# Two V tiles moved from the stage before the attention scores into the filler work between them, the first keys fetched on ScalarE's queue, and another order of the last output tiles

## The chip, the cores and the metric

One core of a Trainium2 chip runs the whole program in one launch. The metric is the device time of one execution in microseconds (us), measured three times; beside it stands one profiled execution, from which all rows below are taken. TensorE is PE in the profile, VectorE DVE, ScalarE ACT, GpSimd POOL and SyncE SP. SP does no arithmetic here; it issues almost all transfers.

## The reference

The input x is 2048 x 512, in float32. The output mixes an attention part and a gated feed-forward part by a gate for each row:

```python
qkv = (x @ wqkv)                      # split into q, k, v: 32 heads of 16 columns each
p = softmax(q @ k.T * 16 ** -0.5)     # 2048 x 2048 for each head
a = (p @ v) @ wo
b = (silu(x @ w1) * (x @ w3)) @ w2    # inner width 1792
g = sigmoid((x * gate_w).sum(-1))
out = g * a + (1 - g) * b
```

## The kernel before

**Precision.** Every float32 product outside the softmax is made of three matmuls on a high and a low half (hi x hi, hi x lo, lo x hi). A V tile (128 rows of x times the V part of `wqkv`, four blocks of 128 inputs) is thus 12 matmuls, in `sums_v`, called by `project_v` (ScalarE copies the result to `V`) or directly.

**The stage before the scores** makes the halves of x, q and k of the first eight heads (stored to DRAM, `store_qk`, and read back by `load_q` and `load_k` into `Qt` and `Kt` with the rows in the order that the score matmuls want), and the 16 V tiles. It also bounds all scores (`bound`), writes the bound to DRAM as guard rows (`guard_rows`, tensor `m_d`) and reads them back under the queries (`load_guard`). A flag from the bound decides at L293 whether a slow exact path (`row_maxima`) is needed. With these inputs it isn't, so every engine jumps over it.

**The branch.** Each engine loads the flag, compares, and jumps. On the path that is taken each engine first waits for its own earlier instructions, and then adds to its semaphores what the skipped path would have added. SP does this for the transfers: it waits until all transfers issued so far have landed, whichever queue issued them, and then counts the eight transfer semaphores up, one after the other. The first score matmul (L829) waits for these counts. Transfers take the eight semaphores (DMAHW0 to DMAHW7 in the rows below) in turn, in the order of the built program with all queues together; one that takes a semaphore waits at its queue until the transfer that had it before has landed.

**The scores.** 1024 units follow, each one score pair (`Q`, two matmuls side by side on 50 rows, L829) and one exponential on ScalarE (L833); the product with V (`P`, L817) comes eight units at a time. Between them stand filler slots (`F`): in one slot `feed` issues one matmul on each half of the array (64 rows each, side by side) from a list of blocks, `blocks()`: the other q and k columns, the feed-forward part, the output projection. A string sets the order. A period `one` has 8 Q, 21 F and 8 units of P, a period `two` 8 Q, 15 F and 8 units of P:

```python
LONG, SHORT = 90, 37
one = "QQFFFFFF" + "QFFF" * 5 + "QPPPP"
two = "QFFF" * 5 + "QPPQQPP"
order = one * LONG + "QQ" + "F" * 7 + two * SHORT + "QFFF" * 5 + "QPPPP"
```

**The end.** After the last P the last two heads are divided by their sums through two rounds of transposes, split into halves, and multiplied with the last block of `wo` (`project`). `mix` then forms `g * a + bt` of one 128-row tile on VectorE and stores it. Output tiles 8 to 15 finish in this stage; of tiles 8 and 10 the scaling runs on ScalarE and the sum on GpSimd (`scaled`).

Of the kernel before, what the change touches and what calls it, by code (L numbers as in the profile page):

```python
# [17 lines left out]
P = 128  # L18
# [4 lines left out]
DH = 16  # L23
NB = S // 512
# [9 lines left out]
def gated_mix_kernel(ctx: ExitStack, tc: tile.TileContext, x, wqkv, wo, w1, w3, w2, gate_w, out):  # L34
# [27 lines left out]
    qkp = ctx.enter_context(tc.tile_pool(name="qkp", bufs=1))  # L62
    fw = ctx.enter_context(tc.tile_pool(name="fw", bufs=2, side="right"))
# [3 lines left out]
    wvp = ph1.enter_context(tc.tile_pool(name="wvp", bufs=1))  # L67
# [330 lines left out]
    bound()  # L398
    project_v(10)
    guard_rows()  # L400
    load_k(0, 0)
    project_v(11)
    x_gate(3)
# [118 lines left out]
    def load_piece(t, q):  # L522
        if t == 1 and q < 2:
            both = wk.tile([P, 2, 512], F32R, name=f"wo{2 + q}")
# [9 lines left out]
    def load_wo(k):  # L534
        if k < 2:
            hi, lo = w2H[3][:, 2 + k, :], w2L[3][:, 2 + k, :]
        else:
            both = wk.tile([P, 2, 512], F32R, name=f"wo{k}")
# [66 lines left out]
    def divide(k, half):  # L605

        yield from reciprocals(k, half)
        for b in (2 * half, 2 * half + 1):
# [4 lines left out]
            else:  # L613
                both = wk.tile([P, 2, 512], F32, name="od")
# [12 lines left out]
    def load_bt(t):  # L627
        bt[t] = wk.tile([P, 512], F32, name=f"bt{t % 3}")
# [62 lines left out]
    def six_heads():  # L691
# [9 lines left out]
        both = wk.tile([P, 2, 512], F32, name="od")  # L701
# [36 lines left out]
    NBLOCK = 8 * len(chunks) + 3 * NT + NT // 2 + NT // 2  # L738
# [4 lines left out]
    halves = [None, None]  # L743
# [7 lines left out]
    def pick(lane, rest, gap):  # L751
# [3 lines left out]
        if used < 0 or over[used] is not None and over[used] + rest <= clock:  # L755
            block, halves[lane] = halves[lane] or next(source, None), None
            if block:
                if type(block[1]) is tuple:
                    product, done, length = block
                    block, halves[1 - lane] = (product, done[0], length), (product, done[1], length)  # L760
                over.append(None)
                return dict(block=block, ps=bank(), id=len(over) - 1, n=0, turn=None, alone=halves[1 - lane] is not None or len(over) == NBLOCK)
# [78 lines left out]
    LONG, SHORT = 90, 37  # L841
# [7 lines left out]
    for i, c in enumerate(order):  # L849
        clock += 1 if c != "P" else 4  # L850
        if c == "Q":
# [14 lines left out]
            if small or later and hurry:  # L866
                for _ in range(3 if hurry else 1 + (len(small) > (6 if len(over) < 8 * len(chunks) - 16 else 0))):
                    if small or later and hurry:
                        (small or later).pop(0)()
            if loads and (hurry or issued % 2 or len(over) > 8 * len(chunks) - 12):  # L870
                loads.pop(0)()
# [44 lines left out]
    project(last, 1, (0, 1))  # L916
# [8 lines left out]
    project(last, 1, (2,))  # L925
    project(last, 2)

    def scaled(t):
        y = wk.tile([P, 512], F32, name=f"p{free[t // 2 - 3]}")
        nc.scalar.activation(y, banks[t], AF.Copy, scale=g[:, t:t + 1])  # L930
        nc.gpsimd.tensor_add(bt[t], bt[t], y)

    def store(t):
        nc.sync.dma_start(out[P * t:P * t + P, :], bt[t])

    banks[8], banks[9] = one_[:, 1, :], two_[:, 1, :]
    banks[10], banks[11] = bank(), bank()
    for two in ((8, 9), (10, 11), (12, 13), (14,), (15,)):
        if two[0] == 12:
            banks[12], banks[13], banks[14] = psum2()[:, 0, :], psum2()[:, 0, :], acc  # L940
        for terms in ((0, 1), (2,)):
            for t in two:
                project(t, k, terms)
        for t in two:
            if t in (8, 10):
                scaled(t)
            elif t < last:
# [33 lines left out]
```

## Time and profile before

| | before |
|---|---|
| median of three runs | 1403.72 us (1402.86 to 1403.92) |
| the profiled execution | 1403.71 us |
| its span in the profile | 1401.9 us |
| PE busy | 1393.8 us, 99% of the span |
| ACT busy | 1034.3 us, 74% |
| DVE busy | 486.9 us, 35% |
| POOL busy | 329.3 us, 23% |
| bytes moved by the DMA engines | 141.03 MB |

The span runs from the first to the last recorded instruction; 1.8 us of the execution lie around it. Matmuls are pipelined and their ends are modelled, so PE's 99% says that it seldom stands idle, not that it runs at its peak.

### The profile page before, as it was taken

Reading aid. Unit: us, or ns where it says so; the run is one execution under the profiler, and the core shown is the slowest. Engines: PE = TensorE matmul, PEld = TensorE weight load, DVE = VectorE, ACT = ScalarE, POOL = GpSimd, SP = SyncE. Lnnn points to the kernel's source line nnn. Section 1 sums busy time; section 2 is a strip of 40 time slices with the busy share of each in tenths; the row PEclk is TensorE's granted clock in tenths of the full one; section 3 lists DMA queues with packets and bytes.
Section 4 is the critical chain, followed back from the end, with each engine's and each line's share of the span. In section 5 each row is a group of like instructions: output and inputs, shape, how many; then the busy total and the mean of one; then the engine's idle time right before and its main releaser. Section 6 shows DMA issues by size and latency. Waiting matters only on the chain.

```text
span 1401.9 us, 29019 instructions
## 1 busy us (share of the span) xinstructions
PE 1393.8 (99%) x11497; PEld 826.4 (59%) x11497; DVE 486.9 (35%) x1083; ACT 1034.3 (74%) x1155; POOL 329.3 (23%) x366
## 2 busy tenths in 40 slices
PE   9999999999999999999999999999999999999998
PEld 8866566566566566566566566566555555555554
DVE  5511111564555546555454554511111101111113
ACT  4457677777777777777777777777677887888784
POOL 6123433011011101110110116432344322212312
PEclk9999999999999999999999999999999999999999
DMA  7653554343223423223333236444354453444632
GB/s 209 166 124 94 133 139 113 73 113 77 46 56 85 114 54 76 69 66 93 74 77 74 66 86 165 118 95 91 87 123 105 105 110 77 111 93 110 157 120 78
DMA packets 112479, 141.03 MB, mean 101 GB/s; under 512 B 16276, under 2 KB 70804, under 8 KB 109264
## 3 DMA queue, kind: packets, MB, share of 16 engines
q1 hardware_dynamic: 111616, 137.92, 41.4%
q8 instruction: 93, 1.52, 0.5%
q10 hardware_dynamic: 720, 1.18, 0.2%
q14 instruction: 50, 0.41, 0.1%
HBM read 90.43 MB, written 48.61 MB: 99 GB/s over the span
## 4 chain that ended last, share of the span: by engine, by line
PE 99%; DVE 0%; issue 0%; DVEq 0%
PE acc L817 33%; PE f L432 27%; PE S L829 19%; PE f L550 11%; PE f L634 2%; PE S L199 2%; PE f L641 1%; PE f L96 1%; PE f L98 1%; PE f L97 1%; PE f L165 0%; PE acc L353 0%; PE f L897 0%; PE S L165 0%; PE S L897 0%; DVE xL L646 0%
## 5 line engine op out<-in xcount | busy, mean ns | idle before, releaser
L833 ACT ACTIVATE p<-S 128x1024 f32<-128x1024 f32 x1024 | 967.9, 1026 | 314.1 <-PE S L829 305.0
L817 PE MATMUL acc<-p,V 128*17 128x512 f32 x4096 | 471.5, 594 | 0.0
L829 PE MATMUL S<-Qt,Kt 50*128 50x512 f32 x2048 | 403.7, 407 | 0.8 <-DVE V L415 0.8
L829 PEld LDWEIGHTS S<-Qt,Kt 50*128 50x128 f32 x2048 | 184.0, 184 | 173.5 <-issue 77.7
L817 PEld LDWEIGHTS acc<-p,V 128*17 128x17 f32 x4096 | 103.4, 97 | 275.2 <-issue 275.2
L463 DVE RECIPROCAL sg<-sg 128x64 f32<-128x64 f32 x448 | 209.2, 517 | 52.7 <-issue 49.1
L432 PE MATMUL f<-xH,fl 64*128 64x512 f32 x1088 | 220.6, 395 | 0.0
L432 PE MATMUL f<-xL,fh 64*128 64x512 f32 x1088 | 219.6, 393 | 0.0
L432 PE MATMUL f<-xH,fh 64*128 64x512 f32 x1088 | 218.0, 389 | 0.0
L328 POOL CAST fh<-fr 128x512 fp32r<-128x512 f32 x34 | 22.4, 658 | 428.0 <-DMA fr<-in_B_w_dram 279.6
L432 PEld LDWEIGHTS f<-xH,fh 64*128 64x128 f32 x1088 | 105.6, 184 | 25.0 <-issue 0.4
L432 PEld LDWEIGHTS f<-xL,fh 64*128 64x128 f32 x1088 | 106.4, 186 | 22.5
L432 PEld LDWEIGHTS f<-xH,fl 64*128 64x128 f32 x1088 | 106.1, 186 | 22.7
L789 DVE MEMSET tick<- 1x1 f32 x198 | 11.7, 59 | 281.2 <-PE f L550 143.0
L455 DVE COPY gs<-f 128x512 f32<-128x512 f32 x56 | 38.5, 688 | 65.5 <-PE f L432 59.3
L461 DVE TENSOR_SCALAR sg<-sg 128x512 f32<-128x512 f32 x56 | 27.3, 488 | 88.0 <-ACT sg L460 84.3
L550 PE MATMUL f<-xH,fh 64*128 64x512 f32 x208 | 57.5, 392 | 0.0
L550 PE MATMUL f<-xH,raw 64*128 64x512 f32 x192 | 57.0, 392 | 0.0
L550 PE MATMUL f<-xL,fh 64*128 64x512 f32 x208 | 56.2, 392 | 0.0
L550 PE MATMUL f<-xH,fl 64*128 64x512 f32 x208 | 55.4, 392 | 0.0
L513 POOL CAST fh<-sg 128x512 fp32r<-128x512 f32 (+1 forms) x32 | 18.0, 563 | 147.3 <-DMA sg<-h_d 91.0
L799 DVE COPY u<-acc 128x512 f32<-128x512 f32 x31 | 21.4, 692 | 86.1 <-PE acc L817 86.1
(202 smaller groups left out, 1324.6 us busy)
## 6 DMA issues: line engine op xcount, KB each, us to landing
Kt<-kH_d SPq DMA_DIRECT2D x128, 128.0 KB
h_d<-sg SPq DMA_DIRECT2D x56, 256.0 KB
sg<-h_d SPq DMA_DIRECT2D x43, 256.0 KB
fr<-in_B_w_dram SPq DMA_DIRECT2D x42, 256.0 KB
Qt<-qH_d SPq DMA_DIRECT2D x128, 64.0 KB
Kt<-kL_d SPq DMA_DIRECT2D x64, 128.0 KB
Qt<-qL_d SPq DMA_DIRECT2D x64, 64.0 KB
b_d<-y SPq DMA_DIRECT2D x16, 256.0 KB
```

The source lines that it names most:

```text
L199: nc.tensor.matmul(ps[:, i, :], w[i][h][:, k, :], xs[b][:, k, :], start=n == 0, stop=n == len(order) - 1)
L328: nc.gpsimd.tensor_copy(hi, src)
L432: return nc.tensor.matmul(ps, w[i == 1][r, k, :], (xL if i == 2 else xH)[b][r, k, :], start=n == 0 and not second, stop=n == 3 * ND - 1 an ...
L455: nc.vector.tensor_copy(gs, ps)
L461: small.append(lambda: nc.vector.tensor_scalar(sg, sg, 1.0, None, op0=OP.add))
L463: small.append(lambda q=q: nc.vector.reciprocal(sg[:, q:q + 64], sg[:, q:q + 64]))
L550: ins = nc.tensor.matmul(ps, hs[t][q][i == 1][r, P * o:P * o + P], (w2L if i == 2 else w2H)[q][r, o, :], start=n == 0 and not second, stop ...
L634: return nc.tensor.matmul(ps, ot[t][i == 1][r, P * k:P * k + P], wo_[k][i == 2][r, :], start=n == 0 and not second, stop=n == 3 * ND - 1 a ...
L799: nc.vector.tensor_copy(u, acc)
L817: nc.tensor.matmul(acc[r:r + DH + 1, :], V[:, k, 2 * j + h, :], p[:, h, :], start=k == 0, stop=k == NT - 1)
L829: nc.tensor.matmul(ps[:, h, :], Kt[i][r:r + 50, P * k:P * k + P], Qt[i][r:r + 50, t:t + 512], start=True, stop=True)
L833: nc.scalar.activation(p, ps, AF.Exp, scale=SCALE)
```

## The change

The diff, cut to its core:

```diff
+EARLY = 14
...
-    def x_gate(b):
-        for t in range(4):
+    def x_gate(b, ts=range(4)):
+        for t in ts:
...
-            vh, vl = (wvp.tile([P, 512], F32R, name=f"v{n}{k}") for n in "hl")
+            both = wvp.tile([P, 2, 512], F32R, name=f"v{k}")
+            vh, vl = both[:, 0, :], both[:, 1, :]
...
-    def load_k(j, i):
+    def load_k(j, i, e=nc.sync):
...
-                nc.sync.dma_start(Kt[i][r + DH * o:r + DH * o + DH, :].bitcast(F32), QD[1][ks][s, :])
+                e.dma_start(Kt[i][r + DH * o:r + DH * o + DH, :].bitcast(F32), QD[1][ks][s, :])
...
     bound()
+    x_gate(3, range(3))
     project_v(10)
     guard_rows()
-    load_k(0, 0)
+    load_k(0, 0, nc.scalar)
+    x_gate(3, range(3, 4))
     project_v(11)
-    x_gate(3)
...
     load_guard(0, 0, 0)
-    project_v(12)
     small = nc.values_load(flag, min_val=0, max_val=1)
-    last_v = [sums_v(t) for t in range(NT - 3, NT)]
+    last_v = [sums_v(t) for t in range(12, EARLY)]
...
+    def v_product(t):
+        b, o = divmod(P * t, 512)
+        def product(ps, r, n, second):
+            k, i = divmod(n, 3)
+            return nc.tensor.matmul(ps, (xL if i == 1 else xH)[b][r, k, o:o + P], wv[k][i == 2][r, :],
+                                    start=n == 0 and not second, stop=n == 3 * ND - 1 and second)
+        return product
+
+    def v_done(t):
+        return lambda ps: nc.vector.tensor_copy(V[:, t, :, 0:DH], ps.rearrange("p (h d) -> p h d", d=DH))
...
+        for t in range(EARLY, NT):
+            yield v_product(t), v_done(t), 3 * ND
         for m, b in turns:
...
-        for t in range(NT // 2, NT - 2):
+        for t in range(NT // 2, NT - 3):
             yield part_product(t, True), part_done(t), LATE
-        yield part_product(NT - 2, False), (part_done(NT - 2), part_done(NT - 2)), LATE
+        for t in (NT - 3, NT - 2):
+            yield part_product(t, False), (part_done(t), part_done(t)), LATE
...
-        if used < 0 or over[used] is not None and over[used] + rest <= clock:
+        if used < 0 or over[used] is not None and over[used] + (rest if len(over) < NBLOCK - 3 else 3) <= clock:
...
-    LONG, SHORT = 90, 37
+    LONG, SHORT = 94, 33
...
-    project(last, 1, (0, 1))
+    project(last, 1)
...
-    project(last, 1, (2,))
-    project(last, 2)
+    project(last, 2, (0, 1))
     banks[8], banks[9] = one_[:, 1, :], two_[:, 1, :]
     banks[10], banks[11] = bank(), bank()
-    for two in ((8, 9), (10, 11), (12, 13), (14,), (15,)):
...
+    project(8, k, (0, 1))
+    project(last, 2, (2,))
+    project(8, k, (2,))
+    mix(8, banks[8])
+    for t in range(9, NT):
+        if t == 12:
             banks[12], banks[13], banks[14] = psum2()[:, 0, :], psum2()[:, 0, :], acc
...
+        project(t, k)
+        if t < last:
+            mix(t, banks[t], nc.scalar if t % 2 else nc.sync)
```

So V tiles 12 and 13 are the last before the branch, and tiles 14 and 15 (24 matmuls of 128 rows) become 48 matmuls of 64 rows, the first blocks of the filler. The string has four more periods `one` and four fewer `two`, which is 24 slots more. The V weights keep their space past the first stage; buffers that were taken anew after the branch (`wo`, `od`, `bt`) now take that space.

The program's rows show three places. The first is SP's queue before the branch; the names are queries `Qt`, keys `Kt`, the guard rows `m_d`, and in brackets the semaphores that a row waits for. Before:

```order
L277 DMA Qt_108<-qH_d 16x1024 [waits DMAHW6_49]
L262 DMA m_d<-sg 32x4x512 [waits DMAHW7_49,DVE_49]
L262 DMA m_d<-sg 32x4x512 [waits DMAHW0_49,DVE_49]
L270 DMA Kt_111<-kH_d 16x2048 [waits DMAHW1_49]
L270 DMA Kt_111<-kH_d 16x2048 [waits DMAHW2_49]
L270 DMA Kt_111<-kL_d 16x2048 [waits DMAHW3_49,Pool_49]
L270 DMA Kt_111<-kH_d 16x2048 [waits DMAHW4_49]
L270 DMA Kt_111<-kH_d 16x2048 [waits DMAHW5_49]
L270 DMA Kt_111<-kL_d 16x2048 [waits DMAHW6_49,Pool_49]
L282 DMA Qt_108<-m_d 2x1024 [waits DMAHW7_49,DMAHW0_49]
L411 TENSOR_LOAD flag [waits DVE_49]
L293 COMPARE_AND_BRANCH
```

The same place of SP's queue in the change:

```order
L279 DMA Qt_108<-qL_d 16x1024 [waits DMAHW7_49]
L279 DMA Qt_108<-qH_d 16x1024 [waits DMAHW1_49]
L264 DMA m_d<-sg 32x4x512 [waits DMAHW2_49,DVE_49]
L264 DMA m_d<-sg 32x4x512 [waits DMAHW4_49,DVE_49]
L284 DMA Qt_108<-m_d 2x1024 [waits DMAHW7_49,DMAHW4_49,DMAHW2_49]
L284 DMA Qt_108<-m_d 2x1024 [waits DMAHW0_49]
L413 TENSOR_LOAD flag [waits DVE_49]
L295 COMPARE_AND_BRANCH
```

And ScalarE's queue in the change, where the six key fetches now stand behind the copy of V tile 10 and ahead of that of V tile 11:

```order
L272 DMA Kt_111<-kH_d 16x2048 [waits DMAHW7_49,DMAHW6_49]
L272 DMA Kt_111<-kH_d 16x2048 [waits DMAHW5_49]
L272 DMA Kt_111<-kL_d 16x2048 [waits DMAHW0_49]
L272 DMA Kt_111<-kH_d 16x2048 [waits DMAHW3_49]
L272 DMA Kt_111<-kH_d 16x2048 [waits DMAHW5_49]
L272 DMA Kt_111<-kL_d 16x2048 [waits DMAHW6_49]
L229 ACTIVATE V<-f 128x32x16 [waits PE_49]
L408 ACTIVATE g<-z 128x16 [waits DVE_49]
L413 TENSOR_LOAD flag [waits DVE_49]
L295 COMPARE_AND_BRANCH
```

The six fetches left SP's queue. The built program lists them between the query fetches, so the semaphores fall otherwise: the first key fetch has DMAHW2, and the first guard write takes DMAHW2 after it, so it waits on SP until that key fetch has landed. Before, it waited for a key store (DMAHW7).

The second place is PE's first work after the branch. Before:

```order
L829 MATMUL S<-Qt_108,Kt_111 128x512 [waits DMAHW2_49,DMAHW3_49,DMAHW1_49,DMAHW5_49,DMAHW0_49,DMAHW6_49,DVE_49,DMAHW7_49,PE_49,Pool_49]
L829 MATMUL S<-Qt_108,Kt_111 128x512 [waits DMAHW2_49,DMAHW1_49,DMAHW4_49,DMAHW0_49,Pool_49]
L829 MATMUL S<-Qt_108,Kt_111 128x512 [waits DVE_49]
L432 MATMUL f<-xH_157,fl_647 128x512 [waits DVE_49,Pool_49]
L432 MATMUL f<-xH_157,fl_653 128x512 [waits DVE_49,Pool_49]
L432 MATMUL f<-xL_158,fh_646 128x512
```

And in the change, where `v` is a V weight:

```order
L852 MATMUL S<-Qt_108,Kt_111 128x512 [waits DMAHW3_49,DMAHW2_49,DMAHW4_49,DMAHW1_49,DMAHW5_49,DMAHW0_49,DMAHW6_49,DVE_49,DMAHW7_49,PE_49,Pool_49]
L852 MATMUL S<-Qt_108,Kt_111 128x512 [waits DMAHW2_49,DMAHW1_49,DMAHW4_49,DMAHW0_49,Pool_49]
L852 MATMUL S<-Qt_108,Kt_111 128x512 [waits DVE_49]
L726 MATMUL f<-v_208,xH_582 128x512 [waits Activation_49]
L726 MATMUL f<-v_208,xH_582 128x512 [waits DVE_49]
L726 MATMUL f<-v_208,xL_583 128x512 x2
```

The first score pair waits for the same counts as before; behind it stand V products where the products for q and k of the next heads stood.

The third place is VectorE's end of program, from the last copy of `acc` on. Before:

```order
L886 COPY u<-acc 128x512
L910 RECIPROCAL recip<-S 128x16
L911 TENSOR_TENSOR p_21172<-S,recip 128x256
L653 SCALAR_TENSOR_TENSOR xL_20232<-f,g,xL_20232 128x512
L924 TENSOR_TENSOR xL_20230<-S,xH_20228 32x512
L924 TENSOR_TENSOR xL_20230<-acc,xH_20228 32x512
L646 SCALAR_TENSOR_TENSOR xH_20231<-S,g,xH_20231 128x512
L646 SCALAR_TENSOR_TENSOR xH_20231<-f,g,xH_20231 128x512
L646 SCALAR_TENSOR_TENSOR xL_20232<-S,g,xL_20232 128x512 x2
L646 SCALAR_TENSOR_TENSOR xL_20232<-acc,g,xL_20232 128x512
L646 SCALAR_TENSOR_TENSOR xL_20232<-f,g,xL_20232 128x256 x2
```

And in the change:

```order
L909 COPY u<-acc 128x512
L933 RECIPROCAL recip<-S 128x16
L934 TENSOR_TENSOR p_21183<-S,recip 128x256
L659 SCALAR_TENSOR_TENSOR xL_20244<-f,g,xL_20244 128x512 x2
L947 TENSOR_TENSOR xL_20242<-S,xH_20240 32x512
L947 TENSOR_TENSOR xL_20242<-acc,xH_20240 32x512
L652 SCALAR_TENSOR_TENSOR xH_20243<-S,g,xH_20243 128x512 x2
L652 SCALAR_TENSOR_TENSOR xH_20243<-f,g,xH_20243 128x512 x2
L652 SCALAR_TENSOR_TENSOR xL_20244<-S,g,xL_20244 128x512 x2
L652 SCALAR_TENSOR_TENSOR xL_20244<-acc,g,xL_20244 128x512
L652 SCALAR_TENSOR_TENSOR xL_20244<-f,g,xL_20244 128x256 x2
```

VectorE has two whole mixes more (tiles 8 and 10), and one more partial sum ahead of them.

## Rows read from the trace of the kernel before

**Rows 1.** Head of the page.

```profile
span 1401.9 us, 29019 instructions
```

**Rows 2.** Timeline of PE at the branch: start, us, line, operation, count [idle before].

```profile
71.88 0.39 PE L96 MATMUL f<-vh,xH 128*128 128x512 f32 x1
...
79.81 0.39 PE L98 MATMUL f<-vh,xL 128*128 128x512 f32 x1
80.97 0.93 PE L829 MATMUL S<-Qt,Kt 50*128 50x512 f32 x4 [0.78 <-DVE V L415]
```

**Rows 3.** Line L293, the branch: ns min/median/max, first and last start in us.

```profile
L293 SPq EVENT_SEMAPHORE  x8: 17/17/17, 78.5 to 79.1; - x8
...
L293 SPq COMPARE_BRANCH  x1: 50/50/50, 75.2 to 75.2; - x1
L293 PEldq COMPARE_BRANCH  x1: 3609/3609/3609, 76.0 to 76.0; - x1
...
L293 PEldq EVENT_SEMAPHORE  x1: 51/51/51, 80.2 to 80.2; - x1
```

**Rows 4.** Timeline of SP before the branch: transfers issued.

```profile
63.49 0.45 SPq L187 DMA_DIRECT2D kL_d<-lo  x1
...
68.23 1.88 SPq L270 DMA_DIRECT2D Kt<-kH_d  x2
...
73.37 0.55 SPq L282 DMA_DIRECT2D Qt<-m_d  x2
```

**Rows 5.** Instructions on the guard rows' tensor `m_d`, 60 to 90 us.

```profile
L262 SPq DMA_DIRECT2D m_d<-sg x2: 316/317/318, 67.3 to 67.9; - x2
```

**Rows 6.** Waits of SP's queue, 60 to 82 us: us in total, times, longest.

```profile
SPq L262 <- DMA kL_d<-lo: 0.2, 1, 0.2
```

**Rows 7.** Timeline of ACT: its copy of V tile 10.

```profile
66.20 0.60 ACT L227 ACTIVATE V<-f 128x512 f32<-128x512 f32 x1 [2.56 <-PE f L98]
```

**Rows 8.** Timeline of SP late: a small store, and the read that needs it.

```profile
1363.58 0.73 SPq L700 DMA_DIRECT2D r_d<-dd  x1
...
1365.60 0.73 SPq L707 DMA_DIRECT2D od<-r_d  x1
```

**Rows 9.** Stretch 70 to 72 us: busy us by engine, PEclk, DMA share, GB/s.

```profile
70.00:72.00 2.00, 2.00 (x10) 1.65 (x10) 1.25 (x5) 0.22 (x1) 0.00 (x0) 1.00 1.21 246
```

**Rows 10.** Stretches at the end, the same columns.

```profile
1396.00:1397.00 1.00, 0.12 (x1) 0.00 (x0) 1.00 (x3) 0.00 (x0) 0.00 (x0) 1.00 1.02 381
...
1398.00:1399.00 1.00, 0.00 (x0) 0.00 (x0) 0.00 (x0) 0.00 (x0) 0.00 (x0) 0.81 1.01 377
```

**Rows 11.** Timeline of PE at the program's start.

```profile
1.55 3.01 PE L353 MATMUL acc<-ident 128*128 128x128 f32 x13 [1.55 <-DVE acc L349]
...
5.54 0.42 PE L165 MATMUL S<-ident,xn 128*128 128x128 f32 x1
...
6.42 0.27 PE L165 MATMUL S<-ident,xn 128*128 128x128 f32 x1
```

**Rows 12.** Chain of work that ended last: P of the periods (start, us).

```profile
88.08 3.56 PE acc L817 x32
...
1023.33 3.56 PE acc L817 x32
...
1034.07 1.84 PE acc L817 x16
...
1373.14 1.84 PE acc L817 x16
```

**Rows 13.** Timeline of DVE at the end.

```profile
1390.61 0.69 DVE L924 TENSOR_TENSOR xL<-acc,xH 32x512 fp32r<-32x512 f32 x1
1392.06 0.75 DVE L646 SCALAR_TENSOR_TENSOR xH<-S,g,xH 128x512 f32<-128x512 f32 x1 [0.77 <-PE S L897]
...
1394.58 1.41 DVE L646 SCALAR_TENSOR_TENSOR xL<-S,g,xL 128x512 f32<-128x512 f32 x2 [0.38 <-PE S L897]
...
1396.56 0.87 DVE L646 SCALAR_TENSOR_TENSOR xL<-f,g,xL 128x256 f32<-128x256 f32 x2
```

More of the change, by code (lines that the diff above doesn't have):

```diff
@@ L523, in load_piece @@
         if t == 1 and q < 2:
-            both = wk.tile([P, 2, 512], F32R, name=f"wo{2 + q}")
+            both = wvp.tile([P, 2, 512], F32R, name=f"v{q}")
             hi, lo = both[:, 0, :], both[:, 1, :]
@@ L537, in load_wo @@
         else:
-            both = wk.tile([P, 2, 512], F32R, name=f"wo{k}")
+            both = wvp.tile([P, 2, 512], F32R, name=f"v{k - 2}")
             hi, lo = both[:, 0, :], both[:, 1, :]
@@ L613, in divide @@
             else:
-                both = wk.tile([P, 2, 512], F32, name="od")
+                both = wvp.tile([P, 2, 512], F32, name="v2")
                 o, r = both[:, 0, :], both[:, 1, :]
@@ L627, in load_bt @@
     def load_bt(t):
-        bt[t] = wk.tile([P, 512], F32, name=f"bt{t % 3}")
+        if t == 0:
+            both = wvp.tile([P, 2, 512], F32, name="v3")
+            bt[-3], bt[-2] = both[:, 0, :], both[:, 1, :]
+            bt[-1] = wk.tile([P, 512], F32, name="bt")[:]
+        bt[t] = bt[t - 3]
         nc.sync.dma_start(bt[t], B_d[P * t:P * t + P, :])
@@ L700, in six_heads @@
         nc.sync.dma_start(rows(R_d), dd[rr])
-        both = wk.tile([P, 2, 512], F32, name="od")
+        both = wvp.tile([P, 2, 512], F32, name="v2")
         pairs = [(both[:, 0, :], both[:, 1, :]), (slot("fr", F32), slot("sg", F32))]
@@ L754, in pick @@
         used = len(over) - 3
-        if used < 0 or over[used] is not None and over[used] + rest <= clock:
-            block, halves[lane] = halves[lane] or next(source, None), None
+        if used < 0 or over[used] is not None and over[used] + (rest if len(over) < NBLOCK - 3 else 3) <= clock:
+            alone = bool(halves[lane])
+            block = halves[lane].pop(0) if alone else next(source, None)
             if block:
@@ L866, in gated_mix_kernel @@
             if small or later and hurry:
-                for _ in range(3 if hurry else 1 + (len(small) > (6 if len(over) < 8 * len(chunks) - 16 else 0))):
+                for _ in range(3 if hurry else 1 + (len(small) > (6 if len(over) < FIRST - 16 else 0))):
                     if small or later and hurry:
                         (small or later).pop(0)()
-            if loads and (hurry or issued % 2 or len(over) > 8 * len(chunks) - 12):
+            if loads and (hurry or issued % 2 or len(over) > FIRST - 12):
                 loads.pop(0)()
@@ L924, in gated_mix_kernel @@
         nc.vector.tensor_sub(Ol[k][rr, a, :], back[a][rr, :], Oh[k][rr, a, :])
-    project(last, 1, (2,))
-    project(last, 2)
[L928 to L934, printed above, removed]
+    project(last, 2, (0, 1))
     banks[8], banks[9] = one_[:, 1, :], two_[:, 1, :]
     banks[10], banks[11] = bank(), bank()
-    for two in ((8, 9), (10, 11), (12, 13), (14,), (15,)):
-        if two[0] == 12:
-            banks[12], banks[13], banks[14] = psum2()[:, 0, :], psum2()[:, 0, :], acc
[L941 to L947, printed above, removed]
-                mix(t, banks[t], nc.scalar if t % 2 == 0 else nc.sync)
-                if t in (9, 11):
-                    store(t - 1)
-            else:
-                mix(t, banks[t], nc.scalar, slice(0, D // 2))
-                mix(t, banks[t], nc.sync, slice(D // 2, D))
+    project(8, k, (0, 1))
[4 more added lines that the diff above has]
+        if t == 12:
+            banks[12], banks[13], banks[14] = psum2()[:, 0, :], psum2()[:, 0, :], acc
+        project(t, k)
+        if t < last:
+            mix(t, banks[t], nc.scalar if t % 2 else nc.sync)
+        else:
+            mix(t, banks[t], nc.scalar, slice(0, D // 2))
+            mix(t, banks[t], nc.sync, slice(D // 2, D))
 _INS = ['A_x', 'A_wqkv', 'A_wo', 'B_w1', 'B_w3', 'B_w2', 'gate_w']
```

12 lines of the change are left out of this document (7 added, 5 removed).

## The prediction

> **What bounds the kernel now.** The span is 1401.9 us in an execution of 1403.71 us [rows 1], which is the median of the three runs to 0.01 us, so the sum below is made against 1403.71. I read the chain of work that ended last first, for the pitch of the periods. From its first P of a period `one` at 88.08 to the ninetieth at 1023.33 lie 89 pitches of 10.51 us; from the first of a period `two` at 1034.07 to the thirty-seventh at 1373.14 lie 36 pitches of 9.42 us [rows 12]. The chain in both is PE's own instructions, so what counts is how many slots PE has to work through, and the two places where it waits: the branch and the end. At the branch I read PE's timeline first: V tiles 13 to 15 run from 71.88 without a gap, the last matmul starts at 79.81 and takes 0.39, and the first score pair starts at 80.97 [rows 2]. The releaser named there, VectorE's copy of V, isn't what PE waits for (the program's first score has no wait for it); it is the branch. So I went to the branch's own line. PE compares at 76.0, ahead of its queued matmuls, and its jump takes 3.6 us; its own count is satisfied at 80.2, when its last V matmul is through. SP compares at 75.2, needs 3.3 us until the first of its eight counts at 78.5, and the last is at 79.1 [rows 3]. SP was thus ready 1.1 us before PE: PE is the late one today, and SP is next. The end I read from VectorE's timeline.
>
> **V tiles off the first stage.** 24 matmuls fewer at the pitch of rows 2, (79.81 - 71.88) / 35 = 0.2266 us, are 5.44 us. PE's last V matmul would be through at 79.81 + 0.39 - 5.44 = 74.8. PE's compare and jump move with its queue, to about 70.6 and 74.2, so they still lie under the matmuls.
>
> **V tiles into the filler.** 24 slots more come by turning four `two` into `one`: 4 x (10.51 - 9.42) = +4.36 us. The 48 half-height matmuls fill these slots, two to a slot, as the other blocks do. The blocks behind them come 24 slots, a little over one period, later until the two strings meet again; what hides that are the transfers' own leads, and if one of them ran out, PE would show a gap between periods, which it doesn't in rows 12.
>
> **When may the first score start?** It needs SP's last count, and SP gets there by a chain: guard writes, guard reads, flag, compare, jump, counts. Before, the first guard read was issued at 73.37 [rows 4], so from there to the last count it is 79.1 - 73.37 = 5.73 us, of which only little depends on landings. In the change the guard reads need the guard writes, and the first guard write needs the first key fetch to have landed. The key fetch can be issued on ScalarE behind its copy of V tile 10, which starts at 66.20 and takes 0.60 [rows 7]: 66.8. For a landing I have two rows. A 256 KB key store issued at 63.49 held up the second guard write, issued at 67.9, for 0.2 us: 4.4 us with the engines full [rows 4 to 6]. A small store issued at 1363.58 had landed when its reader was issued at 1365.60: at most 2.0 us with idle engines [rows 8]. So the guard writes start at 68.8 to 71.2 and, with 0.5 us between the two, the reads are issued between 66.8 + 2.0 + 0.5 + 2.0 = 71.3 and 66.8 + 4.4 + 0.5 + 4.4 = 76.1. For the key fetch, half as large and alone on its ring, I take 2.7; for the two guard writes, which now share the engines with four or five key fetches instead of going ahead of them, 4.4, as it is nearest to the store: 66.8 + 2.7 + 0.5 + 4.4 = 74.4. Nothing else is removed there, and in the stretch from 70 to 72 the DMA share was 1.21 [rows 9], so the same bytes can't be through much sooner. The last count is then at 74.4 + 5.73 = 80.1. PE passes its own waits after that; today this takes 0.77 us in all (80.2 to 80.97), most of it ahead of the last wait, so 0.3. First score: 80.4 instead of 80.97, **-0.6 us** (77.3 to 82.1 by the bounds, -3.7 to +1.1).
>
> On several queues there is a rule that speaks against the change. The row says 246 GB/s at a share of 1.21 with SP's queue alone [rows 9], against 381 GB/s at 1.02 for output stores [rows 10], which leaves room for a second queue to move more. The Trainium skill (DMA: Bandwidth & Descriptors, section Issuing engines are not separate DMA queues) says that transfers of all issuing engines run on the same 16 DMA engines and interleave. By the rule the guard writes are held up by the keys and the sum is the one here; by the room in the row they would be as fast as at idle, which is the second rival below. No run here shows two queues at this place.
>
> **What PE's wait costs.** PE then idles from 74.8 to 80.4, 5.6 us, where it idled 0.78. After the last matmul of the program, over by 1396.12, the granted clock was 1.00 until 1397 and 0.81 on average from 1398 to 1399: it fell from 2.4 to 1.2 GHz in that microsecond, under 3 us after the work ended [rows 10]. At the program's start, matmuls from 1.55 on took 3.01 / 13 = 0.23 us each, single ones 0.42 us at 5.54 and 0.27 us at 6.42 [rows 11]: the clock rose about 4.5 us after the first one. I take the same here: 4.5 us at half the clock do 2.25 us of work, **+2.25 us**; the bounds are 0 (the clock holds) and 2.25. The periods are bound by PE, so this isn't hidden.
>
> The row shows the fall once, at the end, and never with work behind it. The Trainium skill (TensorE: Matmul & The Clock Gate, section Why this matters for your kernels) tells to leave no idle gaps between bursts of matmuls because the clock goes back to half. By this rule the gap costs the 2.25 us; if the end is no model for a gap in the middle, the time is 1406.9, the first rival.
>
> **ScalarE and VectorE at the branch.** ScalarE's copy of V tile 11 and the gate now stand behind six fetches that wait; three of the four gate products moved ahead of the guard rows on VectorE, into its wait for PE there. Both are over before SP's counts, and nothing else stands behind them: 0. If VectorE's jump came after 80.1, the first score would wait for it instead.
>
> **The end.** The first mix followed the last split, which ended at 1390.61 + 0.69 = 1391.30, only at 1392.06; two mixes in a row take 1.41, the last two halves 0.87 [rows 13]. In the change tile 8 is ready when the split ends, so VectorE runs on: 1391.35 + 7 x 0.705 + 0.87 = 1397.2, against 1396.56 + 0.87 = 1397.4, in spite of two more mixes. The first store goes 0.7 us earlier. The stores run near the limit (8 x 256 KB at 381 GB/s are 5.5 us), so they may end up to 0.7 us earlier too. The extra partial sum lies in VectorE's wait before the split. Between 0.2 and 0.7 I take **-0.6 us**, as the transfers were continuous to the end. The halved blocks and the shorter rest only keep the filler dense in the last period: 0.
>
> **Sum:** -0.57 + 2.25 + 4.36 - 0.6 = +5.4; 1403.71 + 5.4 = **1409.1 us**.
>
> **Rivals.** (1) *The clock holds through the gap*: 1409.1 - 2.25 = 1406.9. (2) *The guard rows land as at idle*: first score at 77.3, the gap is 2.5 us and the clock holds: -3.7 + 4.36 - 0.6 = 0, 1403.8. For it speaks the room in rows 9 (246 GB/s where rows 10 have 381). It decides from a guard read issued before about 72.5. (3) *PE goes on when its V tiles end*, since SP's chain shortens with the six fetches gone: -5.44 + 4.36 - 0.6 = -1.7, **1402.0**, on the other side. SP's queue itself would be free at 68; against it speaks the program, in which the guard write waits for a key fetch. It needs the guard read issued at 69.5. (4) *The guard writes come last of all transfers*: first score at 82.1, 1.7 us later than taken: 1410.8.
>
> **How the numbers follow.** 0.2%, 2.8 us, is about what a measurement of this kernel can tell from no change: faster below 1400.9, slower above 1406.5. Forecast 0.56, rival 1 0.15, rival 2 0.16, rival 3 0.06, rival 4 0.07. The range leaves out rival 3 and the far ends: 1403.7 to 1411.2; the likeliest case's own is 1407.5 to 1410.5. Slower holds the forecast, rival 4 and two thirds of rival 1: 0.73. Same holds the rest of rival 1, rival 2 and half of rival 3: 0.23. Faster is what is left: 0.04.
>
> **What would show it.** Right: SP's guard reads issued at 73.5 or later, SP's counts at about 80, PE idle over 5 us before the first score, a lower granted clock behind it; 94 periods `one` at 10.5 and 33 `two` at 9.4; VectorE's mixes without gaps at the end. Wrong: a first score before 78, or a granted clock of 1.00 from 75 to 90.

## The result and the profile after

The changed kernel takes 1409.72 us (median of 6 runs, 1409.44 to 1411.60) against 1403.82 us before (6 runs): a ratio of 1.0045, 95% interval 1.0032 to 1.0058. It is slower by more than the 0.2% that the prediction took for no change, and 0.6 us from the 1409.1 us forecast. The profiled execution took 1409.44 us. That the sum is right to 0.6 us is luck: three of its four terms are off by 0.7 to 1.6 us, and the errors cancel.

The head of the page after:

```profile
span 1407.2 us, 29097 instructions
```

The span grew by 5.3 us [rows 1]. I read the same views as before. First PE's timeline at the branch (start, us, line, operation, count [idle before]):

```profile
73.90 0.39 PE L99 MATMUL f<-v,xL 128*128 128x512 f32 x1
81.96 1.42 PE L852 MATMUL S<-Qt,Kt 50*128 50x512 f32 x4 [7.68 <-SPq L295]
82.95 0.86 PE L726 MATMUL f<-v,xH 64*128 64x512 f32 x2
83.38 0.86 PE L726 MATMUL f<-v,xL 64*128 64x512 f32 x2
...
87.44 0.54 PE L726 MATMUL f<-v,xL 64*128 64x512 f32 x2
87.67 0.53 PE L726 MATMUL f<-v,xH 64*128 64x512 f32 x2
```

V ends 5.9 us earlier than in [rows 2], but the first score is 1.0 us later: PE idles 7.68 us, and the releaser is now SP's branch. The filler behind it runs at a pitch of 0.43 us (82.95 to 83.38), later at 0.23 (87.44 to 87.67). The stretches say why (busy us of PE, PEld, DVE, ACT and POOL, then PEclk, DMA share, GB/s):

```profile
74.00:76.00 2.00, 0.29 (x2) 0.00 (x0) 0.60 (x3) 0.08 (x1) 0.00 (x0) 1.00 0.75 186
76.00:78.00 2.00, 0.00 (x0) 0.00 (x0) 0.00 (x0) 0.00 (x0) 0.00 (x0) 0.60 0.08 27
...
84.00:86.00 2.00, 2.00 (x13) 2.00 (x11) 0.00 (x0) 1.06 (x2) 0.00 (x0) 0.50 0.56 172
86.00:88.00 2.00, 2.00 (x17) 2.00 (x16) 0.00 (x0) 1.49 (x2) 0.00 (x0) 0.84 1.12 164
88.00:90.00 2.00, 2.00 (x18) 1.78 (x17) 0.12 (x2) 2.00 (x3) 0.00 (x0) 1.00 1.04 135
```

The granted clock fell from 1.00 (2.4 GHz) to 0.50 (1.2 GHz) between 76 and 78 and came back to 1.00 between 86 and 88. Why SP was late stands in its own timeline and ScalarE's, and in the branch's line:

```profile
67.64 0.30 SPq L279 DMA_DIRECT2D Qt<-qH_d  x1
71.53 1.81 SPq L264 DMA_DIRECT2D m_d<-sg  x2
76.88 0.57 SPq L284 DMA_DIRECT2D Qt<-m_d  x2
```

```profile
66.20 0.82 ACTq L272 DMA_DIRECT2D Kt<-kH_d  x2
```

```profile
L295 SPq EVENT_SEMAPHORE  x8: 17/17/17, 81.1 to 81.7; - x8
...
L295 PEldq COMPARE_BRANCH  x1: 4332/4332/4332, 70.1 to 70.1; - x1
...
L295 SPq COMPARE_BRANCH  x1: 45/45/45, 78.4 to 78.4; - x1
```

And the waits of SP's queue from 60 to 82 us (us in total, times, longest):

```profile
SPq L264 <- DMA Kt<-kH_d: 3.5, 1, 3.5
SPq L284 <- DMA m_d<-sg: 3.5, 1, 3.5
```

The first key fetch is issued at 66.20. The first guard write (L264) waits 3.5 us for its landing and goes at 71.53; the reads wait another 3.5 us for the writes and go at 76.88; SP's last count is at 81.7. Before, the guard writes went at 67.3 and waited 0.2 us, for a store [rows 3 to 6]. The chain of waits gives the periods. Before, with its last P and the one long period, which the earlier rows left out:

```profile
791.85 3.56 PE acc L817 x32
802.78 2.25 PE acc L817 x17
...
1382.58 1.82 PE acc L817 x13
```

And after:

```profile
91.09 3.56 PE acc L840 x32
...
1067.88 3.56 PE acc L840 x32
1078.60 1.41 PE acc L840 x11
...
1389.25 3.56 PE acc L840 x32
```

So the 5.3 us split in three. First P: 91.09 - 88.08 = +3.01, of which the first score's lateness is 0.99 and the rest, 2.02, the slow clock. From the first P to the last: 1298.16 - 1294.50 = +3.66. From the last P to the end: (1407.2 - 1389.25) - (1401.9 - 1382.58) = 17.95 - 19.32 = -1.37. VectorE runs through the end without the gaps of [rows 13], as forecast:

```profile
1397.51 0.69 DVE L947 TENSOR_TENSOR xL<-acc,xH 32x512 fp32r<-32x512 f32 x1
1398.23 1.41 DVE L652 SCALAR_TENSOR_TENSOR xH<-S,g,xH 128x512 f32<-128x512 f32 x2
...
1402.96 0.88 DVE L652 SCALAR_TENSOR_TENSOR xL<-f,g,xL 128x256 f32<-128x256 f32 x2
```

Of the -1.37, though, only 0.26 is there when the last mix ends (14.59 us behind the last P, against 14.85 before). The other 1.1 lies behind it, where only the last stores run.

### The profile page after: what moved, and what is told of

It reads as the page before. It is cut to its first block, busy times and chain, and to the rows that moved or that the text cites. A ratio compares the mean times of both kernels' runs of the same rounds, so it can differ in the third digit from the quotient of the medians.

```text
span 1407.2 us, 29097 instructions
## 1 busy us (share of the span) xinstructions
PE 1393.6 (99%) x11521; PEld 827.7 (59%) x11521; DVE 490.9 (35%) x1088; ACT 1032.3 (73%) x1152; POOL 326.8 (23%) x364
## 4 chain that ended last, share of the span: by engine, by line
PE 94%; DVE 0%; DVEq 0%; issue 0%
PE acc L840 33%; PE f L434 27%; PE S L852 19%; PE f L552 11%; PE f L640 2%; PE f L647 1%; PE f L726 1%; PE f L920 0%; PE S L920 0%; DVE xL L652 0%; PE acc L920 0%; PE S L944 0%; PE acc L944 0%; PE S L931 0%; DVEq L986 0%
## 5 line engine op out<-in xcount | busy, mean ns | idle before, releaser
L434 PE MATMUL f<-xH,fl 64*128 64x512 f32 x1088 | 219.3, 395 | 0.0
L434 PE MATMUL f<-xL,fh 64*128 64x512 f32 x1088 | 218.4, 393 | 0.0
L552 PE MATMUL f<-xL,fh 64*128 64x512 f32 x208 | 66.5, 392 | 0.0
L552 PE MATMUL f<-xH,fl 64*128 64x512 f32 x208 | 66.3, 392 | 0.0
L571 DVE SCALAR_TENSOR_TENSOR y<-f,omg,y 128x512 f32<-128x512 f32 x32 | 24.1, 752 | 112.9 <-PE f L552 112.9
L552 PE MATMUL f<-xH,raw 64*128 64x512 f32 x192 | 53.9, 392 | 0.0
```

Of the source, the lines that this page charges most:

```text
L434: return nc.tensor.matmul(ps, w[i == 1][r, k, :], (xL if i == 2 else xH)[b][r, k, :], start=n == 0 and not second, stop=n == 3 * ND - 1 an ...
L552: ins = nc.tensor.matmul(ps, hs[t][q][i == 1][r, P * o:P * o + P], (w2L if i == 2 else w2H)[q][r, o, :], start=n == 0 and not second, stop ...
L571: nc.vector.scalar_tensor_tensor(y, ps, omg[:, t:t + 1], y, op0=OP.mult, op1=OP.add)
```

## The experiments

Ten runs in three groups. Each has its own ratio to the kernel before on the same chip, whose medians there were 1403.61, 1403.57 and 1403.81 us. Each has one trace, of one of its executions. The traces differ by up to 1.4 us in when the first stage gets going, ahead of every edit of these runs: ScalarE's first split of q and k starts at 15.22 (keys on GpSimd) to 16.58 (guard rows direct, 16 transposes), in the change at 15.26 and before it at 15.76. A later first score is the edit's doing only as far as it exceeds that.

### The first keys on SP's queue again

```diff
-    load_k(0, 0, nc.scalar)
+    load_k(0, 0)
```

> The change with one edit: the first keys are fetched on SP's queue again, behind the guard writes. Theory A (the first guard write is held by the landing of the first key fetch): SP issues the guard writes at about 69 and the first guard read at about 73, as before the change (73.4, less the 0.5 us by which everything ahead is earlier now), the first score is at about 79 instead of 82.0, PE still idles some 4.7 us, so the granted clock still falls; 1409.7 - 3.0 = about 1406.7. Rival B (the guard rows are late because the transfers around them fill the engines, whichever queue fetches the keys): first score at 81.5 or later, 1409.3 to 1409.7. Rival C (the shorter wait lets the clock hold): first score at 79 and granted clock 1.00, 1406.7 - 2.3 = 1404.4.

1407.18 us, ratio 1.0024 (1.0013 to 1.0034). SP's and PE's timelines, and the branch's line:

```profile
66.77 0.90 SPq L264 DMA_DIRECT2D m_d<-sg  x2
...
71.56 0.55 SPq L284 DMA_DIRECT2D Qt<-m_d  x2
```

```profile
79.04 1.42 PE L852 MATMUL S<-Qt,Kt 50*128 50x512 f32 x4 [4.80 <-SPq L295]
```

```profile
L295 SPq EVENT_SEMAPHORE  x8: 17/17/17, 78.3 to 78.8; - x8
...
L295 SPq COMPARE_BRANCH  x1: 50/50/50, 73.4 to 73.4; - x1
```

Theory A: the guard writes go 4.8 us earlier and the first score comes 2.9 us earlier, at 79.04, with the clock falling as before. Of the 4.8 us only 2.9 arrive, as SP took 4.9 us from its compare to its first count (73.4 to 78.3) where the change's took 2.7. Theory C is out.

### The first keys on GpSimd's queue

```diff
-    load_k(0, 0, nc.scalar)
+    load_k(0, 0, nc.gpsimd)
```

> The change with the first keys fetched on GpSimd's queue: the guard writes then wait for no key fetch, but the keys still go beside them or ahead of them on the same 16 engines. Theory A (the wait for a landing is the cause): guard writes issued at about 69, first guard read at 73 to 74, first score at 79 to 79.5, 1406.7 to 1407.2. Rival B (sharing the engines is the cause): guard writes issued early, but the guard read is issued at 76 or later and the first score is at 81.5 or later, 1409.3 or more.

1406.93 us, ratio 1.0024 (1.0015 to 1.0034).

```profile
66.75 0.90 SPq L264 DMA_DIRECT2D m_d<-sg  x2
73.42 0.57 SPq L284 DMA_DIRECT2D Qt<-m_d  x2
```

```profile
78.22 1.15 PE L852 MATMUL S<-Qt,Kt 50*128 50x512 f32 x4 [4.00 <-SPq L295]
```

The first score is at 78.22, behind 4.00 us of idle time. The keys still share the engines with the guard rows, but SP no longer waits for a key fetch to land, and the first score comes 3.7 us earlier than in the change. The wait is the cause, not the sharing. The sharing has a price of its own: the guard writes took 6.7 us here until their reader was issued, 4.8 with SP's queue in order. The profiled execution is the fastest of the ten (1404.95), 2.0 us under their median, and has a mean granted clock of 0.999 where eight of the others have 0.998; so up to 2 us of what this trace shows may be its own, and the time rests on the median.

### Work in PE's wait, 26 transposes

```diff
+    idle(26)
     row_maxima(small)
```

> The change with 26 transposes of the identity into the unused accumulator bank behind V tile 13, at 0.22 us each some 5.7 us of work that leads to nothing, so that PE isn't idle while it waits for SP. Theory A (the fall of the granted clock costs 2.3 us): first score still at 82.0, granted clock 1.00 throughout, first P of the chain at about 89 instead of 91.1, time 1409.7 - 2.3 = 1407.4. Rival (the slow stretch isn't the clock, or what it costs is made up later): first P as in the change, or the same time of 1409.7 within 0.6. Rival 2 (the transposes delay PE's own jump): first score after 82.5 and 1408 to 1410.

1409.27 us, ratio 1.0040 (1.0026 to 1.0054), and the test failed to make its condition: the transposes took 0.115 us each, not 0.22, so PE still idled.

```profile
74.91 3.00 PE L355 MATMUL acc<-ident 128*128 128x128 f32 x26
82.24 1.42 PE L853 MATMUL S<-Qt,Kt 50*128 50x512 f32 x4 [4.33 <-SPq L295]
```

The granted clock was 0.80 on average from 80 to 82 and 0.50 from 82 to 88. First P at 91.84. The first score is 0.3 us later than in the change, less than the 0.8 us by which this trace starts later. So it decides nothing on the clock, and was made again with 48.

### Work in PE's wait, 48 transposes

```diff
+    idle(48)
     row_maxima(small)
```

> The change with 48 transposes of the identity behind V tile 13 instead of the 26 of the earlier run, which took 0.115 us each and left 4.3 us of idle time, behind which the granted clock fell all the same. At 0.115 us, 48 fill 5.5 us, until about 80.3, so that PE idles at most 2 us. Theory A (the fall of the clock is what the wait costs beyond its own length): granted clock 1.00 until the filler runs, first score at 82 to 82.5, first P of the chain at 89.3 to 89.8 instead of 91.8, 1409.3 - 2.2 = about 1407.1. Rival (the slow stretch isn't the clock, or is made up later): first P as with 26, or a time within 0.7 of 1409.3. Rival 2 (the longer queue holds up PE's own jump): first score after 82.8 and about 1408.

1408.51 us, ratio 1.0034 (1.0021 to 1.0046).

```profile
75.16 5.40 PE L355 MATMUL acc<-ident 128*128 128x128 f32 x48
83.42 0.93 PE L853 MATMUL S<-Qt,Kt 50*128 50x512 f32 x4 [2.86 <-PEq L295]
```

```profile
82.00:84.00 2.00, 0.57 (x5) 0.54 (x6) 0.00 (x0) 0.00 (x0) 0.00 (x0) 1.00 0.21 47
84.00:86.00 2.00, 2.00 (x20) 1.85 (x18) 0.00 (x0) 1.71 (x2) 0.00 (x0) 1.00 0.36 96
```

Theory A: the clock held at 1.00, and the first P came 90.54 - 83.42 = 7.12 us after the first score, as before the change (88.08 - 80.97 = 7.11), where the change needs 9.13. Of rival 2 there is a part: PE's own jump now ends last, at 82.7 against 82.6 for SP's last count (the releaser is PE's queue). The first score is 1.5 us later than in the change, but 1.1 of that is the later start of this trace (16.34 against 15.26). By the medians, each against the kernel before on its chip, 1.0 of the 2.0 us is gained: +4.9 against +5.9.

### The new end alone

The kernel before with the new last part: all V tiles ahead (with the change's names), keys on SP's queue, gate products where they were. The edit against the change, cut:

```diff
-EARLY = 14
+EARLY = 16
...
+    project_v(12)
...
-    last_v = [sums_v(t) for t in range(12, EARLY)]
+    last_v = [sums_v(t) for t in range(13, EARLY)]
...
-    LONG, SHORT = 94, 33
+    LONG, SHORT = 90, 37
```

> The kernel before with the new last part alone: all 16 V tiles ahead of the first score, keys on SP's queue, gate products where they were, 90 and 37 periods, but the extra partial sum, the halved blocks and the tile-by-tile mixes on VectorE of the change. Theory A (the end gives 1.4 us, as the two traces compare it: 19.34 us from the start of the last P to the end of the span before, 17.95 after): 1403.8 - 1.4 = 1402.4, and nothing else changes. Rival (the end gives the 0.6 us that I had predicted, the rest of the shorter end comes from the blocks that the change had moved): 1403.2. Rival 2 (the end gives nothing by itself): 1403.8.

1403.59 us, ratio 1.0000 (0.9991 to 1.0009): rival 2, no gain that the runs can tell, though a gain of up to 1.3 us isn't excluded. The median span is 0.4 us shorter than before (1401.4 against 1401.8 on that chip), and 0.4 us more lies outside it (2.2 against 1.8). In the trace the last P is at 1382.13, the last mix starts at 1395.85 (13.72 us later; 13.71 in the change), but the span ends 19.27 us after the P. Stretches of this run, and then of the change at about the same distance from its last P:

```profile
1398.00:1399.00 1.00, 0.00 (x0) 0.00 (x0) 0.00 (x0) 0.00 (x0) 0.00 (x0) 1.00 0.40 147
1399.00:1400.00 1.00, 0.00 (x0) 0.00 (x0) 0.00 (x0) 0.00 (x0) 0.00 (x0) 1.00 0.05 16
```

```profile
1405.00:1406.00 1.00, 0.00 (x0) 0.00 (x0) 0.00 (x0) 0.00 (x0) 0.00 (x0) 1.00 0.47 168
1406.00:1407.00 1.00, 0.00 (x0) 0.00 (x0) 0.00 (x0) 0.00 (x0) 0.00 (x0) 1.00 0.00 0
```

The mixes are as early, but the DMA engines are still busy, at a share of 0.05, in a microsecond in which they are idle in the change.

### The old end in the change

```diff
-        for t in (NT - 3, NT - 2):
-            yield part_product(t, False), (part_done(t), part_done(t)), LATE
+        yield part_product(NT - 2, False), (part_done(NT - 2), part_done(NT - 2)), LATE
...
-    for t in range(9, NT):
+    for two in ((8, 9), (10, 11), (12, 13), (14,), (15,)):
```

> The change with the old last part: no extra partial sum, one halved block, the pairs of tiles with ScalarE and GpSimd in the mixes, the old rule for a block's start. All else as in the change. Theory A (the new end gives nothing by the clock of the runs, as in the run of the new end alone): 1409.7. Rival (the new end is worth the 1.4 us that the traces of the change and of before differ by, when V tiles 14 and 15 are in the filler): 1411.1. Rival 2 (my forecast's 0.6): 1410.3.

1411.33 us, ratio 1.0057 (1.0044 to 1.0071): 1.6 us above the change, nearest to the rival's number (1411.1). From last P to span end it is 1409.5 - 1389.15 = 20.35 us, 1.0 more than before the change. PE's timeline has a part of it, filler that is left over behind the last P:

```profile
1392.64 0.50 PE L647 MATMUL f<-xH,xH 64*128 64x512 f32 x1
...
1394.22 0.50 PE L917 MATMUL f<-xH,xH 128*128 128x512 f32 x1
```

Six slots in a single half (1.58 us), where before two took 0.66 and in the change three pairs take 0.89. The halved blocks and the shorter rest, which I had put at 0, take 0.7 us of leftovers away here.

### V tiles 14 and 15 in both places

The run of the new end alone, with tiles 14 and 15 computed again as the first filler, and 94 and 33 periods. The edit against the change, cut:

```diff
-    load_k(0, 0, nc.scalar)
...
+    load_k(0, 0)
...
+    project_v(12)
...
-    last_v = [sums_v(t) for t in range(12, EARLY)]
+    last_v = [sums_v(t) for t in range(13, NT)]
```

> V tiles 14 and 15 are computed twice: all 16 ahead of the first score, with SP's key fetch and the gate products where they were, as in the run of the new end alone, and 14 and 15 a second time as the first blocks of the filler, with 94 and 33 periods. So the start is that of the kernel before and the filler that of the change. Theory A (24 more slots in the filler cost what the two traces show, 1298.16 - 1294.50 = 3.7 us from the first P of the chain to the last, whatever the start does): first P at 87.7, last P 1298.2 later, 1403.6 + 3.7 = 1407.3, or 1405.9 if the end is also 1.4 shorter, as in the trace of the change. Rival (the longer filler costs that only because it starts late and on a slow clock): 1294.5 to 1296, about 1403.6 to 1405. Rival 2 (my forecast's four pitches): 1298.9, 1408.

1407.30 us, ratio 1.0027 (1.0016 to 1.0038), 3.7 above the run of the new end alone. First P 87.72, last 1387.02: 1299.30, which is 1.1 more than in the change, in some nine periods of 10.6 instead of 10.5; the end is 17.98. So the first rival is out: behind an early start and a full clock the 24 slots cost no less than in the change, here 4.8 us from first P to last (1299.30 against 1294.47 with the new end alone), nearer to my forecast's four pitches (1298.9). That the time is theory A's 1407.3 all the same is luck, as the end took 1.3 us off. The shorter end goes with the 94 and 33 periods and the V tiles in the filler, which no run parts, and not with the start.

### The guard rows without their trip through memory

The keys on GpSimd's queue, and the first step's guard rows copied from the rows in SBUF into the query tile; the guard writes stay for the later steps, the reads ahead of the branch go.

```diff
+            for h in range(2):
+                nc.sync.dma_start(Qt[0][64 * h + 48 + a:64 * h + 49 + a, :].bitcast(F32).rearrange("p (j t) -> p j t", t=512),
+                                  r[a][h:h + 1, :].bitcast(F32)[:, None, :].to_broadcast([1, 2, 512]))
...
-    load_guard(0, 0, 0)
```

> The change with the first keys on GpSimd's queue and the first step's guard rows copied straight from the rows in SBUF into the query tile (four small transfers ahead of the two guard writes), so that SP reads no guard row back before the branch. Theory A (the trip of the guard rows out and back sets SP's readiness): SP compares at 70 to 71.5 instead of 75.0 to 78.4, its last count comes at 74 to 76.5, the first score at 75 to 77, PE idles 1 to 2.7 us, the clock holds, first P at 82.8 to 84.8, and the time is 1403.6 + (84 - 88) + 3.7 = about 1403, 1401.5 to 1404.5. Rival B (the counts still wait for the two guard writes, or the jump waits for the full engines): first score at 78 and 1406 to 1407. Rival C (PE's own jump, which took 6.3 us with the keys on GpSimd's queue, comes last): first score at 77, clock 1.00, 1404 to 1405.

1405.88 us, ratio 1.0015 (1.0006 to 1.0024). The branch's line:

```profile
L299 SPq EVENT_SEMAPHORE  x8: 17/17/17, 77.1 to 77.7; - x8
...
L299 PEldq COMPARE_BRANCH  x1: 6548/6548/6548, 70.5 to 70.5; - x1
...
L299 SPq COMPARE_BRANCH  x1: 45/45/45, 72.5 to 72.5; - x1
...
L299 PEldq EVENT_SEMAPHORE  x1: 51/51/51, 77.1 to 77.1; - x1
```

SP compares 2.5 us earlier than with the trip (75.0), but then takes 4.6 us to its first count, and the first score is at 77.94: rival B. Of rival C only this is there, that PE's jump takes 6.5 us and ends 0.6 us ahead of SP's last count (77.1 and 77.7). So the trip isn't the last thing in the way; SP's jump is, or the transfers that its counts wait for (DMA share 0.91 from 72 to 74, 0.56 from 74 to 76), which this run doesn't part. PE idled only 3.26 us, and the clock fell all the same; the first P came 9.85 us after the first score.

### The same with 16 transposes

```diff
+    idle(16)
     row_maxima(small)
```

> The run with the guard rows copied straight from SBUF and the keys on GpSimd's queue (1405.9, first score at 77.9, slow clock behind it until 84.2, first P at 87.8), with 16 transposes of the identity behind V tile 13, 1.8 us of work that leads to nothing. Theory A (the parts add up: start, clock, 24 more slots, end): PE idles under 2.5 us, the clock holds, first score at 77.7 to 78.9, first P 7.1 later, at 84.8 to 86.0, the filler 3.7 longer, the end as in the change: 1405.9 - 2.7 + (0 to 1) = 1403.2 to 1404.2, no faster than the kernel before. Rival (the clock falls all the same, as with 26 transposes in the change): 1405.9. Rival 2 (with the wait gone the move is a gain after all): below 1402.2.

1404.96 us, ratio 1.0009 (1.0000 to 1.0018). The clock held; first score 79.86, first P 87.23, 7.37 later. The first score is 1 us later than I expected, and 0.9 of that is the start of this trace (16.58 against 15.69): the guard copies went at 68.09 instead of 67.21. PE's jump ended last, at 79.0. Even here the move doesn't win.

### All V tiles ahead, keys on ScalarE's queue

```diff
-EARLY = 14
+EARLY = 16
...
-    LONG, SHORT = 94, 33
+    LONG, SHORT = 90, 37
```

> The change with V tiles 14 and 15 ahead of the first score again and 90 and 37 periods; the first keys stay on ScalarE's queue, the gate products ahead of the guard rows, the new end. It is the run of the new end alone (1403.6) plus the key fetch on ScalarE's queue. Theory A (the fetch holds up SP's chain and with it the first score, whatever PE does): guard read issued at 76.5 to 77.4 instead of 72.9, SP's last count at 81.7 instead of 78.5, so PE, through with its V tiles at 79.8, waits for it: first score at 82 instead of 80.5, an idle time of about 2 us in which the clock holds, first P at 89.1 instead of 87.7, 1405.1. Rival (with PE busy until 79.8 the later chain is hidden): 1403.6. Rival 2 (the clock falls after 2 us of idle time too): 1407.

1404.59 us, ratio 1.0003 (0.9994 to 1.0012). Guard reads at 76.98, SP's last count at 81.7, first P at 89.16, 1.5 us later than in the run of the new end alone. The first scores, of this run and then of the new end alone:

```profile
82.03 0.94 PE L853 MATMUL S<-Qt,Kt 50*128 50x512 f32 x4 [1.04 <-DVE V L418]
```

```profile
80.56 0.93 PE L852 MATMUL S<-Qt,Kt 50*128 50x512 f32 x4 [0.78 <-DMA Qt<-qH_d]
```

That looks like theory A, but 1.2 of the 1.5 us is the later start of this trace (16.57 against 15.31): PE's last V matmul starts at 80.60 against 79.39. What the later counts add is the difference in idle time, 1.04 - 0.78 = 0.3 us. So the first rival is right but for 0.3 us: with PE busy, its cover hides the fetch. The medians are 1.0 us apart, within the intervals.

## Why the prediction was right, and where it wasn't

| run | first split | idle before the first score | first score | first P | first P less first score | first P to last |
|---|---|---|---|---|---|---|
| before | 15.76 | 0.78 | 80.97 | 88.08 | 7.11 | 1294.50 |
| after | 15.26 | 7.68 | 81.96 | 91.09 | 9.13 | 1298.16 |
| keys on SP | 15.26 | 4.80 | 79.04 | 87.98 | 8.94 | 1298.17 |
| keys on GpSimd | 15.22 | 4.00 | 78.22 | 87.04 | 8.82 | 1298.20 |
| 26 transposes | 16.05 | 4.33 | 82.24 | 91.84 | 9.60 | 1298.19 |
| 48 transposes | 16.34 | 2.86 | 83.42 | 90.54 | 7.12 | 1298.42 |
| guard rows direct | 15.69 | 3.26 | 77.94 | 87.79 | 9.85 | 1298.18 |
| the same, 16 transposes | 16.58 | 2.55 | 79.86 | 87.23 | 7.37 | 1298.18 |
| new end alone | 15.31 | 0.78 | 80.56 | 87.66 | 7.10 | 1294.47 |
| V tiles in both places | 15.46 | 0.72 | 80.59 | 87.72 | 7.13 | 1299.30 |
| all V tiles ahead, keys on ScalarE | 16.57 | 1.04 | 82.03 | 89.16 | 7.13 | 1294.49 |

**When the first score may start** (-0.57 taken, +0.99 measured): the mechanism was right, the size wrong. The step that failed is "for the key fetch, half as large and alone on its ring, I take 2.7". It was issued at 66.20, and the guard write that waits for it at 71.53: up to 5.3 us, more than the 4.4 that I had as the upper end. The DMA share was 1.04 from 66 to 68 and 0.99 from 68 to 70, full of what SP had issued ahead of it. A ring of its own didn't help. That is the rule cited there from the Trainium skill (DMA: Bandwidth & Descriptors, section Issuing engines are not separate DMA queues): the transfers of all issuing engines interleave on the same 16 DMA engines. The row on room for more, 246 against 381 GB/s, was no sign of a faster landing. Two errors in the other direction hid half of it: the whole start of this trace runs 0.5 us earlier than before (ScalarE's first split at 15.26 instead of 15.76, its copy of V tile 10 at 65.72 instead of 66.20), which the split shows ahead of all work that the change moved, and from the guard read to the last count it took 4.8 us instead of 5.73. Less that start, the first score is 1.5 us later than before, not 1.0. Undoing the fetch's queue in two ways gave 2.9 and 3.7 us back at the first score, 2.5 and 2.8 us of time. Most of PE's wait is there without the fetch (4.80 us of idle time with the keys on SP's queue), and with all V tiles ahead the same fetch delayed the first score by 0.3 us. Rival 2 is out; the first score came where rival 4 had it (82.1), and the total is below that rival's 1410.8 by what the other terms fell short.

**What PE's wait costs** (+2.25 taken): 9.13 - 7.11 = 2.02 measured, and gone where PE was kept busy and the clock held (7.12). Rival 1 is out. For the cost, the model was fair. Its second half, though, wasn't read from the clock: the profile's granted clock is 1.00 at the program's start (0 to 8 us), so that those first matmuls ran at half the clock was argued from their length. The cost doesn't grow with the wait: 2.7 us behind 3.26 us of idle time, 1.7 behind 4.00, 2.0 behind 7.68. It goes with how much work met the low clock. With the guard rows direct the granted clock was 0.50 all the way from 78 to 84, behind a first score at 77.94. With the keys on GpSimd it was still 1.00 from 76 to 78 and 0.85 from 78 to 80, so it fell only behind the first score (78.22), and from 82 to 84 it was at 0.80 again.

**V tiles into the filler** (+4.36 taken, +3.66 measured): the pitches held, 10.503 (976.79 / 93) and 9.414 (310.65 / 33), and their difference is 1.09. What I overlooked is that the kernel before had a period of 10.93 at 791.85 that the change hasn't; that is 0.43 of the missing 0.70. Rows 12, by which I took it that no period has a gap, show only the ends of the two strings. Another 0.16 is the pitch into the last P, 9.28 instead of 9.44. The long period comes back with 90 and 37 periods (also at 791.42 with the new end alone). Its cause wasn't followed up.

**The end** (-0.6 taken): -1.37 in the two traces, 0.0 by the runs of the new end alone, -1.6 as the difference between the old and the new end in the change. The mixes ran as forecast (0.26 us earlier), but the rest of the gain is behind them, so that the sign came out right was in part luck. What I missed is the leftover filler, which the moved tiles lengthen under the old rules. Why the last transfers are drawn out with 90 and 37 periods stays open.

**Off the sum**: outside the span 2.24 us instead of 1.81, +0.43, a term that the sum didn't have. It isn't chance: the six executions of the change have 2.21 to 2.30, those of the kernel before on all chips 1.75 to 1.92. It goes with the new end (2.19 to 2.32 with that end alone, 1.75 to 1.83 with the old end in the change), though not where GpSimd fetches the keys (1.74 to 1.85). Its cause stays open. The classes' chances, added up from their parts, are 0.73, 0.24 and 0.03, not 0.73, 0.23 and 0.04.

The rival on the other side, that PE goes on when its V tiles end, wasn't reached by any of these edits. With tiles 14 and 15 gone from the start 5.44 us of PE's work are saved there and 3.7 come back in the filler, so that even with no wait at all the move would give 1.7 us. The best start that I found, 77.94, is 3.0 us earlier than before, and with a full clock that would be less than the 3.7 that the filler takes. No version beat the kernel before by more than the runs can tell; the new end alone equals it.

## What to carry to other kernels

Work taken off an engine ahead of a branch is worth only what the next engine's readiness allows: look for who comes second, and for what its queue waits, before moving work. A transfer put on another queue can hold up the queue it left, if that one's next transfer now has to wait for its landing; price that landing at what other transfers took while the engines were full. And an idle PE cost more than its idle time here, since the work behind it ran at half the clock for some microseconds; filling the gap cured that, but the longer queue ahead of the branch delayed PE's own jump. Before a first score or a first product is compared between two traces, look whether the traces already differ ahead of the edit.

## What the runs showed of the hardware

The time from a compare to the jump's end isn't of one length. SP's, from compare to first count, took 4.9 us when begun at 73.4 (keys on SP), 4.6 at 72.5, 3.3 at 75.2 [rows 3], 2.7 at 78.4 (the change) and 2.5 at 75.0 (keys on GpSimd); PE's took 6.5 us begun at 70.5 (guard rows direct), 4.3 at 70.1 (the change) and 3.8 at 75.8 (26 transposes). ScalarE's and GpSimd's took under 0.6 us in every run. Those of SP and PE begun while the DMA share was near 1 (1.07 from 70 to 74 with the keys on SP) are mostly the long ones, and those at 0.03 (78 to 80 in the change) the short ones. SP's counts also wait for all transfers to land, so its times may hold some of that. PE waits there only for its own instructions, and the DMA view shows what is under way meanwhile, in the change (70.1 to 74.4) and with the guard rows direct (70.5 to 77.0), as packets, MB and share of the 16 engines:

```profile
q8 instruction: 1, 0.02, 2.2%
```

```profile
q8 instruction: 1, 0.02, 1.1%
```

In all twelve traces one 16 KB packet of this queue lies between PE's compare and the end of its jump, and the jump ends 1.3 to 1.6 us after it. What varies is when the packet starts: 1.0 us behind the compare before, 1.4 in the change (71.44), 2.5 with the keys on SP, 3.9 with the guard rows direct (74.39). The Trainium skill (Runtime: NRT & Kernel Launch, section Instruction fetch mechanics) says that a taken branch whose target isn't at hand fetches it by DMA before it goes on. The trace agrees for PE, with this packet. That the fetch starts late because the engines are full fits the order of these runs, but no run here changed the load alone, so it is argued, not shown. It would explain why each gain in SP's chain was partly given back.

The transposes behind V tile 13 took 3.00 / 26 = 0.115 us each, at a granted clock of 1.00. I had expected the 0.23 us of those at the program's start [rows 11]. The granted clock reads 1.00 there too, so why those took twice as long isn't shown.
